# A two-layer FFT mixer and feed-forward kernel on one core: changed end wait, FFN rows 2 and 3 in half-height matmuls, smaller evictions and loads, and a new hand-made order

## Chip, cores and metric

The kernel runs on one core of one Trainium2 chip. The metric is the device time of one execution in microseconds, as the median of several runs. TensorE is PE in the profile, VectorE is DVE, ScalarE is ACT, GpSimdE is POOL, and SyncE is SP, which here issues nearly all the DMAs.

## What is computed

`x` has 2048 tokens of 448 features in bf16. Two identical layers follow one another, each a spectral mixing step and a feed-forward step:

```python
def _A_ref(x, w_r, w_i):
    X = rfft2(x.astype(float32), axes=(-2, -1))
    X = X * (w_r + 1j * w_i)
    return irfft2(X, s=(S, D), axes=(-2, -1)).astype(bfloat16)

def _B_ref(x, w1, b1, w2, b2):
    h = einsum("bsd,df->bsf", x, w1) + b1          # 448 -> 1792
    h = where(h > 0, h, 0) ** 2
    return einsum("bsf,fd->bsd", h, w2) + b2       # 1792 -> 448

x = x + _A_ref(layernorm(x), w_r, w_i)
x = x + _B_ref(layernorm(x), w1, b1, w2, b2)
x = x + _A_ref(layernorm(x), w_r, w_i)
x = x + _B_ref(layernorm(x), w1, b1, w2, b2)
```

The layer norms have no learned scale. The weights are the same in both layers and stay in SBUF.

## The kernel before

**Tiles and stages.** The 2048 tokens are 16 tiles of 128 rows, `x_sb[:, t, :]`, with row p*16+t in partition p. All transforms are matmuls with constant matrices that are loaded from DRAM (`TD`, `G`, `H`, `TI`, `FI`, `FA`, `J`). A layer runs through these stages, and the tag of each is the name used in the text:

- **A1.t / A2.t** (first layer / second layer, tile t). Statistics for the layer norm (`ln_stats`), the cosine/sine matrix scaled by 1/std (`scaled` into `Fs`), four matmuls, and an eviction of the PSUM bank (128x512) to `XA` (`A_out`). In A1 the input comes from `xin`, which is loaded in the pieces listed in `XLOADS`. In A2 the input tile is x as the first layer leaves it. It is folded first into sums and differences (`tt` into `xin`, then into `yA`), so that each of the four matmuls takes 112 of the folded columns.
- **TD.p**, p from 1 to 15 and then 0: four matmuls (in layer 2 four times 112 wide) that need `XA` of all 16 tiles, and an eviction.
- **B.p**: three matmuls of 448 columns with `G_sb[:, p]`, eviction to `EF`.
- **W.p**: the complex product with the spectral weights `Wt` on DVE, as one multiplication into `tmp`, one subtraction and one sum into `Z`, for one p or two at once.
- **Bi.p**: four matmuls of 128 rows and 256 columns with `H_sb[:, p]`, eviction to `VT`. TI of any tile needs all 16 of them.
- **TI.t, AI.t**: the last inverse transform, per tile, and its addition to `x_sb`.
- **ln.t, xbln.t**: square and square root on ACT, then the tile is transposed to `yT` for the FFN. Tiles 0 and 1 are transposed on PE with a permutation matrix `J_sb` (`flip`). The others go by a DMA transpose. Tiles 0 to 3 are not normalised: the raw x is transposed, the mean and the standard deviation ride along in two more columns, which meet two rows b1 in `W1_sb`, and the result is scaled by `r2` afterwards. Tiles 4 to 15 are normalised into `xn` (`scaled`, and a copy `cp` of the last 64 columns) and then transposed.
- **h.c.t0**: the first FFN matmul of chunk c (four tiles). Chunk 0 is done in two parts of two tiles each by `h_part`: per block of 128 hidden features (14 blocks) four matmuls of 128 rows and 256 columns. Chunks 1 to 3 are done by `h_pairs`: every 128-row block is cut into two halves of 64 rows, of which two at a time run side by side in the upper and the lower half of the array. The 448 input features are seven halves per block of hidden features, so 98 halves a chunk with N=512. The last 64 rows of W1 must stand in the upper partitions for that. They are loaded again into `W1u`. Then squared ReLU: ACT does ReLU with the bias `b1col`, DVE squares.
- **o.t**: 14 matmuls of 448 columns and one DVE instruction that adds the residual. Tile 15 is done in two column parts in layer 1 (`CUT`, 224 and 224) and three in layer 2.
- **Output**: a DMA per tile or part, issued by SP. At its end the program waits for each of SP's DMA semaphores. SP's DMAs use 20 semaphores in turn.

**What sets the order.** The code records operations in units, and `ORDER`, a table written by hand, gives each unit its rank. A letter behind the rank (a, d, p) gives the engine. Each engine then executes its own list in rank order and waits on semaphores where an operand isn't ready yet, so an early instruction that waits holds all that stand behind it on its engine. This holds for SP too: a DMA that waits for its target buffer to be free holds every DMA behind it.

**Lines.** In the trace of before all matmuls are L637, activations L656, evictions L662 (ACT) and L663 (DVE), `scaled` L673/L674, DVE two-input operations L689, copies L693, DMAs L628, DMA transposes L623, statistics L788 to L795, the addition in AI L938, the square L962, the output of o L1060, and the filler matmuls that keep TensorE's clock up L1153. The waits at the end are L1166.

## Time and profile before

| | us |
|---|---|
| median of 3 runs | 258.3 |
| lowest, highest | 258.0, 259.23 |
| the profiled execution, its time | 258.49 |
| the profiled execution, span of the trace | 256.7 |
| PE busy | 247.8 (97%) |
| DVE busy | 203.1 (79%) |
| ACT busy | 167.5 (65%) |
| granted TensorE clock | 1.00 |

The trace covers one execution. Its time is 1.8 us more than its span, since the time has work ahead of and behind the recorded instructions in it. A row of the timeline gives start, length, engine, line, and operation, then out<-in with shapes, and how many such instructions in a row it stands for. In square brackets is the idle time ahead of it and what ended it. The trace shortens names, so that `W_sb` is W1_sb or W2_sb and `in_B_b_dram` is b1 or b2. SPq is SP's sequencer, which issues DMAs.

### The profile page before, as it was taken

How to read it: one execution, taken by the hardware profiler on the slowest of the kernel's cores; microseconds unless marked ns; L12 is line 12 of the kernel's file. 1: busy time of each engine (PE TensorE's matmuls, PEld its weight loads, DVE VectorE, ACT ScalarE, POOL GpSimd, SP SyncE). 2: the span in 40 equal slices, each digit the busy share in tenths (PEclk: the TensorE clock that was granted, in tenths of full speed). 3: DMA queues.
4: the chain of work that ended last, by engine and by line, in shares of the span. 5: the costliest groups of instructions: out<-in, count | busy, mean ns of one | idle time of the engine just before them, and what ended most of it. 6: DMA issues, size and time to landing. Idle time of an engine off the chain costs nothing.

```text
span 256.7 us, 5442 instructions
## 1 busy us (share of the span) xinstructions
PE 247.8 (97%) x2025; PEld 155.0 (60%) x2025; DVE 203.1 (79%) x622; ACT 167.5 (65%) x397; POOL 6.5 (3%) x18
## 2 busy tenths in 40 slices
...
GB/s 235 308 181 307 174 224 6 99 233 36 44 3 40 43 43 72 4 0 0 3 0 3 1 3 0 3 43 43 42 72 3 41 63 106 46 3 0 58 38 67
DMA packets 30397, 17.25 MB, mean 67 GB/s; under 512 B 23170, under 2 KB 28898, under 8 KB 30372
## 3 DMA queue, kind: packets, MB, share of 16 engines
...
## 4 chain that ended last, share of the span: by engine, by line
PE 80%; ACT 12%; DVE 3%; DMA 3%; issue 1%; SPq 0%; POOL 0%
PE ps L637 79%; ACT arena L662 5%; ACT VT L662 5%; DMA xin<-in_A_x_dram 3%; ACT tmp L662 1%; DVE x_sb L938 1%; DVE XA L663 1%; SPq L628 0%; ACT VT L962 0%; DVE Fs L674 0%; DVE tmp L663 0%; DVE st L788 0%; PE ps L1153 0%; DVE x_sb L1060 0%; POOL Fs L674 0%
## 5 line engine op out<-in xcount | busy, mean ns | idle before, releaser
L637 PE MATMUL ps<-yT,W_sb 64*128 64x512 bf16 (+1 forms) x770 | 89.8, 346 | 0.0
L637 PE MATMUL ps<-W_sb,arena 128*128 128x448 bf16 (+2 forms) x490 | 87.5, 336 | 0.0
L637 PEld LDWEIGHTS ps<-yT,W_sb 64*128 64x128 bf16 (+1 forms) x770 | 50.7, 95 | 36.9 <-issue 1.5
L637 PEld LDWEIGHTS ps<-W_sb,arena 128*128 128x128 bf16 x490 | 46.2, 98 | 36.7 <-DVE arena L689 1.0
L656 ACT ACTIVATE arena<-ps,b1col 128x512 bf16<-128x512 f32 x84 | 52.3, 691 | 19.3 <-PE ps L637 19.1
L689 DVE TENSOR_TENSOR arena<-arena 128x512 bf16<-128x512 bf16 (+1 forms) x140 | 45.4, 368 | 14.1 <-ACT arena L656 13.9
L962 ACT ACTIVATE VT<-x_sb 128x448 bf16<-128x448 bf16 x32 | 18.3, 574 | 15.5 <-DVE x_sb L938 15.4
L662 ACT ACTIVATE arena<-ps 128x448 bf16<-128x448 f32 x54 | 25.5, 608 | 2.7 <-PE ps L637 2.7
L1060 DVE SCALAR_TENSOR_TENSOR x_sb<-ps,arena 128x448 bf16<-128x448 f32 (+2 forms) x27 | 15.3, 570 | 14.6 <-PE ps L637 14.3
L656 ACT ACTIVATE mv<-mv,epst 128x1 f32<-128x1 f32 (+1 forms) x46 | 13.0, 296 | 13.6 <-DVE mv L789 12.9
L656 ACT ACTIVATE arena<-ps 128x256 bf16<-128x256 f32 x56 | 17.6, 397 | 0.8 <-PE ps L637 0.7
L689 DVE TENSOR_TENSOR tmp<-arena,Wt 128x1792 bf16<-128x1792 bf16 (+1 forms) x20 | 17.7, 903 | 0.2
L637 PE MATMUL ps<-H_sb,arena 128*128 128x256 bf16 x128 | 15.8, 272 | 0.3 <-ACT VT L662 0.3
L637 PE MATMUL ps<-yT,VT 64*128 64x512 bf16 x42 | 15.8, 376 | 0.0
L637 PE MATMUL ps<-arena,G_sb 128*128 128x224 bf16 (+1 forms) x96 | 15.7, 290 | 0.0
L662 ACT ACTIVATE XA<-ps 128x512 bf16<-128x512 f32 x28 | 15.0, 607 | 1.0 <-PE ps L637 0.8
L662 ACT ACTIVATE VT<-ps 128x512 bf16<-128x512 f32 (+2 forms) x28 | 14.6, 808 | 0.0
L637 PEld LDWEIGHTS ps<-H_sb,arena 128*128 128x128 bf16 x128 | 11.7, 98 | 3.2 <-DVE arena L689 0.8
L637 PE MATMUL ps<-TD_sb,XA 128*128 128x224 bf16 (+1 forms) x128 | 12.1, 236 | 0.9 <-DVE XA L663 0.7
L689 DVE TENSOR_TENSOR arena<-tmp 128x448 bf16<-128x448 bf16 (+1 forms) x40 | 11.7, 341 | 0.1
L938 DVE SCALAR_TENSOR_TENSOR x_sb<-ps,mv,x_sb 128x448 bf16<-128x448 f32 x16 | 10.7, 679 | 1.3 <-PE ps L637 1.3
L637 PE MATMUL ps<-TI_sb,VT 112*128 112x112 bf16 (+1 forms) x128 | 9.7, 224 | 1.8 <-ACT VT L662 1.5
...
## 6 DMA issues: line engine op xcount, KB each, us to landing
out_dram<-x_sb SPq DMA_DIRECT2D x15, 112.0 KB, 1.8
...
G_sb<-c_G SPq DMA_DIRECT2D x3, 480.0 KB, 6.1
H_sb<-c_H SPq DMA_DIRECT2D x3, 480.0 KB, 8.8
...
```

The source lines that it names most:

```text
L637: return sch.add("pe", lambda e: e.matmul(_res(o), lhsT, rhs, start=start, stop=stop, skip_group_check=skip), [lhsT, rhs], [o], cost=cost, ...
L656: sch.add("act", lambda e: e.activation(o, _res(i), func, **kw), rd, [o], cost=c)
L662: op = sch.add(engs[0], lambda e: e.activation(o, _res(i), ACT.Copy) if h[0].eng == "act" else e.tensor_copy(o, _res(i)), [i], [o], cost=c ...
L663: e.tensor_copy(o, _res(i)), [i], [o], cost=c[engs[0]], unit=unit)
L689: sch.add(eng, lambda e: e.tensor_tensor(o, _res(a), b, op), [a, b], [o], cost=_free(o) / rate + 69.0)
L938: small(lambda e, xx=xx, xi=xi, r=r, m=m: e.scalar_tensor_tensor(out=xx, in0=_res(r), scalar=m, in1=xi, op0=ALU.subtract, op1=ALU.add), [r ...
L962: sch.add("act", lambda e, i=i, o=o, x=x: e.activation(o, x, ACT.Square, accum_out=mv[:, i, 4:5]), [x], [o, mv[:, i, 4:5]], cost=560.0)
L1060: small(lambda e: e.scalar_tensor_tensor(out=o, in0=_res(i), scalar=r[0] if r else 1.0, in1=xb[:, t, d0:d1], op0=ALU.mult, op1=ALU.add), [ ...
```

## The change

1. **End.** The semaphores of the DMAs are awaited in the order of their last use, so the last transfer is awaited last. Before, they were awaited by index, and the last transfer's was the twelfth of 20.
2. **FFN rows 2 and 3** (the second half of chunk 0). In both layers `h_pairs` is used for them (`NORM0 = (2, 2)`), with N=256. So 98 halves of 64 rows take the place of 56 matmuls of 128 rows. Tiles 2 and 3 are normalised for that like tiles 4 to 15. The upper copy of the last W1 rows comes from a new DMA of 64x1792 into `XA[64:128]` (`W1f`), once per layer. `XA` is read by all TD of the layer before it is free.
3. **Tile 15 in A2.** The output of layer 1 for tile 15 comes in 336 and 112 columns instead of 224 and 224 (`LAST`). The second fold of this tile is done on TensorE (`PFOLD`), and the first fold is cut into pieces of 112 columns.
4. **Evictions.** Those to `XA` of tiles 12 to 15 (layer 1) and of 13 and 15 (layer 2) are cut into two halves. Those to `VT` for some p are cut into a part for 4 tiles and a part for 12, which may come later (`A_CUT`, `BI_CUT`). Before, the latter was done for p=0 alone.
5. **W.** In layer 2 the sum is left out for p = 11 to 15 and 0 (`NOZI`): two sums of two p and two of one p. Bi multiplies the two addends one after the other with the same `H_sb`, so that it has six matmuls instead of four for these six p, 12 matmuls of 256 columns more.
6. **Loads and small buffers.** x is loaded in smaller pieces over the queues of SP and ACT. `J_sb` has a tile of its own, and some small tiles are merged.
7. **Order.** The whole of `ORDER` is new.

In the diff below only the entries of Bi0.0 and TI0.0 in `ORDER` are left, and the passing on of arguments is left out.

```diff
-XLOADS = (("sp", ((0, 1, 3300.0), (2, 4, 4450.0), (4, 6, 5900.0), (8, 12, 7500.0))),
-          ("act", ((None, None, 3150.0), (1, 2, 4600.0), (6, 8, 6100.0), (12, 16, 8500.0))))
+XLOADS = (("sp", ((0, 1, 3200.0), (2, 4, 4700.0), (4, 6, 5950.0), (8, 10, 7200.0), (12, 14, 8700.0))),
+          ("act", ((None, None, 3000.0), (1, 2, 4850.0), (6, 8, 6150.0), (10, 12, 7400.0), (14, 16, 8900.0))))
 NP = 16
-BI_CUT = (0,)
+BI_CUT = ((0, 10, 12, 13), (0, 3, 10, 11))
+NORM0 = (2, 2)
+A_CUT = ((12, 13, 14, 15), (13, 15))
+LAST = 336
+PFOLD = (15,)
+NOZI = ((), (11, 13, 15, 0))
...
-    "Bi0.0": "264 265a 270a", "TI0.0": "267 268d 269 271d 279 280a 272 274d", "AI0.0": "277 278",
...
+    "Bi0.0": "275 276a 278a", "TI0.0": "279 280a 281 282d 293 294d 286 287a", "W1f0": "223", "AI0.0": "285 288",
...
+        W1f = XA[:].rearrange("p a b c t j -> p (a b c t j)")[:, 0:2048].rearrange("p (k c) -> p k c", k=4)
...
-        J_sb = x_sb[:, 4:6, D:4 * P]
+        J_sb = sb("J_sb", [P, P])
...
-        def evac(o, i, engs=("act", "dve"), unit=None):
+        def evac(o, i, engs=("act", "dve"), unit=None, after=None):
...
+            if after is not None:
+                op.deps.append(after)
+                op.gdeps.append(after)
...
-        def A_out(t, q, engs):
-            src = q[lambda b: ps[:, b, :].rearrange("p (k c j) -> p k c j", k=4, c=2 * NP)]
-            dst = XA[:, :, :, :, t, :].rearrange("p k g c j -> p (k g) c j")
-            evac(dst, src, engs)
+        def A_out(t, q, engs, cut):
+            prev = None
+            for a, b in ((0, NP), (NP, 2 * NP)) if cut else ((0, 2 * NP),):
+                src = q[lambda x, a=a, b=b: ps[:, x, :].rearrange("p (k c j) -> p k c j", k=4, c=2 * NP)[:, :, a:b]]
+                dst = XA[:, :, :, a:b, t, :].rearrange("p k g c j -> p (k g) c j")
+                evac(dst, src, engs, after=prev)
+                prev = sch.last_write[_pages(dst)[0]]
...
-            tt(z[:, :, 1], T[:, :, 0, 1], T[:, :, 1, 0], ALU.add)
+            if p in NOZI[L]:
+                for k in range(n):
+                    parts[L, p + k] = (T[:, k, 0, 1], T[:, k, 1, 0])
+            else:
+                tt(z[:, :, 1], T[:, :, 0, 1], T[:, :, 1, 0], ALU.add)
...
-                for h in range(2):
-                    mm(q[lambda b, lb=lb: ps[:, b, lb * 256:(lb + 1) * 256]], Z[:, p, h, lb:256:2],
-                       H_sb[:, p, P * (1 - h):P * (1 - h) + 256], h == 0, h == 1, skip=True)
+                mm(q[lambda b, lb=lb: ps[:, b, lb * 256:(lb + 1) * 256]], Z[:, p, 0, lb:256:2], H_sb[:, p, P:P + 256],
+                   True, False, skip=True)
+                zs = parts.get((L, p), (Z[:, p, 1],))
+                n = QD if len(zs) == 2 else P
+                for i, z in enumerate(zs):
+                    mm(q[lambda b, lb=lb, n=n: ps[0:n, b, lb * 256:(lb + 1) * 256]], z[:, lb:2 * n:2], H_sb[:, p, 0:256],
+                       False, i == len(zs) - 1, skip=True)
...
-            for a, b in ((0, 4), (4, NT)) if p in BI_CUT else ((0, NT),):
-                evac(VT[:, :, :, a:b, 2 * p:2 * p + 2, :].rearrange("p a g t c j -> p (a g) t (c j)"),
-                     q[lambda b0, a=a, b=b: ps[:, b0, :].rearrange("p (k t c) -> p k t c", k=4, t=NT)[:, :, a:b]], EV["Bi"])
+            prev = None
+            for a, b in ((0, 4), (4, NT)) if p in BI_CUT[L] else ((0, NT),):
+                dst = VT[:, :, :, a:b, 2 * p:2 * p + 2, :].rearrange("p a g t c j -> p (a g) t (c j)")
+                evac(dst, q[lambda b0, a=a, b=b: ps[:, b0, :].rearrange("p (k t c) -> p k t c", k=4, t=NT)[:, :, a:b]], EV["Bi"],
+                     after=prev)
+                prev = sch.last_write[_pages(dst)[0]]
...
-            if t < 4:
+            if plain:
...
-                for i in range(n):
-                    scaled(xn[:, i, 0:D], x_sb[:, t + i, 0:D], rstd[:, t + i, 0:1], EV["XN"])
-                cp(xn[:, 0:n, D:4 * P], xn[:, 0:n, 3 * P:D])
-                dma("sp", yT[:, t:t + n, :, :].rearrange("p t k c -> p (t k) c"),
-                    xn[:, 0:n, :].rearrange("p t c -> p (t c)"), transpose=True, lat=2000.0 if t == 4 and not last else 400.0)
+                for i in range(t, t + n):
+                    scaled(xn[:, i % 2, 0:D], x_sb[:, i, 0:D], rstd[:, i, 0:1], EV["XN"])
+                    if t < NFLIP:
+                        flip(i, 1, 0, 4, lambda i: xn[:, i % 2, :])
+                if t >= NFLIP:
+                    cp(xn[:, 0:n, D:4 * P], xn[:, 0:n, 3 * P:D])
+                    dma("sp", yT[:, t:t + n, :, :].rearrange("p t k c -> p (t k) c"),
+                        xn[:, 0:n, :].rearrange("p t c -> p (t c)"), transpose=True, lat=2000.0 if t == 4 and not last else 400.0)
...
-        def h_pairs(c):
-
-            tk = slice(4 * c, 4 * c + 4)
+        def h_pairs(c, t0, t1, W1u):
+
+            tk, w = slice(4 * c + t0, 4 * c + t1), (t1 - t0) * P
...
-                w = W1u[h, fb // 4, fb % 4 * P:(fb % 4 + 1) * P] if up and j == 3 else W1_sb[h, j, f]
-                op = mm(q[fb][lambda b: ps[:, b, :]], w, yT[h, tk, j, :], start, stop, unit=u)
+                s = W1u[h, fb // 4, fb % 4 * P:(fb % 4 + 1) * P] if up and j == 3 and max(NORM0) else W1_sb[h, j, f]
+                op = mm(q[fb][lambda b: ps[:, b, 0:w]], s, yT[h, tk, j, :], start, stop, unit=u)
...
-                    hb = hbuf[c % 2][:, fb, :]
-                    act(hb, q[fb][lambda b: ps[:, b, :]], ACT.Relu, bias=b1col[:, fb:fb + 1])
+                    hb = hbuf[c % 2][:, fb, t0 * P:t1 * P]
+                    act(hb, q[fb][lambda b: ps[:, b, 0:w]], ACT.Relu, bias=b1col[:, fb:fb + 1])
...
+            n = 2 * P if t in PFOLD else P
+            f = Fs[:, t % NFS, 0:n]
+            scaled(f, FA_sb[:, 0:n], rstd[:, t, 0:1], EV["FS2"])
             q = _Tile(1)
-            for k in range(2):
+            for g in range(2) if t in PFOLD else ():
+                w = xin[:, t, g * HD:(g + 1) * HD]
+                for k, (a, m) in enumerate(((w[:, 0:QD], f[:, None, 0:P].to_broadcast([P, 2, P])),
+                                            (w[:, QD:HD], f.rearrange("p (k c) -> p k c", k=2)))):
+                    mm(q[lambda b, g=g: ps[0:QD, b, :].rearrange("p (k g c) -> p g k c", k=2, g=2)[:, g]], a, m,
+                       k == 0 and g == 0, k == 1 and g == 1, skip=True)
+            for k in range(2) if t not in PFOLD else ():
                 for g in range(2):
                     d = (2 * k + g) * QD
                     mm(q[lambda b, d=k * 2 * P + g * P: ps[:, b, d:d + P]], yA[:, t % 8, d:d + P], f,
                        k == 0 and g == 0, k == 1 and g == 1, skip=True)
-            A_out(t, q, EV["A2"])
+            A_out(t, q, EV["A2"], t in A_CUT[1])
...
-        CUT = ((0, HD), (HD, D)) if HALVES else ((0, D),)
+        CUT = ((0, LAST), (LAST, D)) if HALVES else ((0, D),)
...
+            if NORM0[L] < 4 and max(NORM0):
+                sch.tag = f"W1f{L}"
+                dma("sp", XA[64:128].rearrange("p a b c t j -> p (a b c t j)")[:, 0:FF], B_w1[384:448, :])
...
+                    if t0 >= NORM0[L]:
+                        h_pairs(c, t0, t1, W1f)
+                        continue
...
+                        for i in (1, 0) if t in PFOLD or t == NT - 1 and LAST > HD else (2,):
+                            if i and t in PFOLD:
+                                a, b = x[:, HD - 1:QD - 1:-1], x[:, HD:HD + QD]
+                            else:
+                                lo, hi = ((0, QD), (QD, HD), (0, HD))[i]
+                                a, b = x[:, lo:hi], x[:, D - 1 - lo:D - 1 - hi:-1]
+                            lo, hi = ((0, QD), (QD, HD), (0, HD))[i]
+                            for g in range(2):
+                                tt(w[:, g, lo:hi], a, b, ALU.subtract if g else ALU.add)
+                        for k in range(2) if t not in PFOLD else ():
...
-            for j in range(_Sched.NDSEM[ename]):
-                fin = sch.final[(ename, True, j)]
-                if fin > 0:
-                    need((ename, True, j), fin)
+            last = {op.dsem: i for i, op in enumerate(sch.ops[ename]) if op.is_dma}
+            for j in sorted(last, key=last.get):
+                need((ename, True, j), sch.final[(ename, True, j)])
```

Three places of the engines' lists follow, before and after. On SP, the DMAs around the second half of the loads of constants; `H_sb` 128x1920 is H for five p, `H_sb` 128x384 H for p=0, `XA<-in_B_w1_dram` the new load. Before:

```order
L628 DMA x_sb<-c_J 128x2x64
L628 DMA Wt<-in_A_w_r_dram 64x6x224
L628 DMA H_sb<-c_H 128x384
L628 DMA G_sb<-c_G 128x1920
...
L628 DMA H_sb<-c_H 128x1920 x3
L628 DMA b1in<-in_B_b1_dram 128x14x1
L628 DMA W1_sb<-in_B_b1_dram 1x1792
L628 DMA Wt<-in_A_w_i_dram 64x224
L628 DMA Wt<-in_A_w_r_dram 64x224
L628 DMA x_sb<-in_B_b2_dram 128x7x64
L628 DMA W1_sb<-in_B_w1_dram 128x3x1792
```

After:

```order
L634 DMA XA<-in_B_w1_dram 64x1792
L634 DMA W1_sb<-in_B_b1_dram 1x1792
L634 DMA Wt<-in_A_w_r_dram 64x224
L634 DMA H_sb<-c_H 128x1920
L634 DMA b1in<-in_B_b1_dram 128x14x1
L634 DMA x_sb<-in_B_b2_dram 128x7x64
L634 DMA J_sb<-c_J 128x128
L634 DMA H_sb<-c_H 128x384
L634 DMA W1_sb<-in_B_w1_dram 128x3x1792
L634 DMA W2_sb<-in_B_w2_dram 128x14x448
```

H for p=0 and J have moved from ahead of the G loads to behind b2row, the third H load stands by itself, and all of these stand behind the new load, which needs `XA` free.

On PE, the first FFN matmuls of rows 2 and 3 in layer 1 and what follows. `yT,W1_sb` is an h matmul, `tmp,FI_sb` and `TI_sb,VT` are stages of TI of later tiles, and `W2_sb,arena` is o. Before:

```order
L637 MATMUL ps<-tmp,FI_sb 128x2x112 x4
L637 MATMUL ps<-yT,W1_sb 128x256 x48
L637 MATMUL ps<-TI_sb,VT 128x112 x8
L637 MATMUL ps<-yT,W1_sb 128x256 x20
L637 MATMUL ps<-tmp,FI_sb 128x2x112 x4
L637 MATMUL ps<-W2_sb,arena 128x448 x28
```

After:

```order
L643 MATMUL ps<-yT,W1_sb 128x256 x16
L643 MATMUL ps<-tmp,FI_sb 128x2x112 x4
L643 MATMUL ps<-yT,W1_sb 128x256 x7
L643 MATMUL ps<-yT,XA 128x256
L643 MATMUL ps<-yT,W1_sb 128x256 x7
L643 MATMUL ps<-yT,XA 128x256
L643 MATMUL ps<-yT,W1_sb 128x256 x13
...
L643 MATMUL ps<-yT,W1_sb 128x256 x12
L643 MATMUL ps<-TI_sb,VT 128x112 x8
L643 MATMUL ps<-W2_sb,arena 128x448 x14
```

The matmuls with `XA` are the halves on the upper copy of W1. In this layer, the first, the 98 halves stand in one piece.

On ACT, the end of A2, with the last evictions to `XA` and the first of TD. Before:

```order
L662 ACTIVATE XA<-ps 128x128x4 x2
L656 ACTIVATE mv<-mv,epst 128x1
L662 ACTIVATE XA<-ps 128x128x4 x4
L662 ACTIVATE arena<-ps 128x448 x23
```

After:

```order
L668 ACTIVATE XA<-ps 128x128x4 x2
L662 ACTIVATE mv<-mv,st 128x1
L668 ACTIVATE XA<-ps 128x128x4 x3
L668 ACTIVATE XA<-ps 128x4x16x4 x4
L668 ACTIVATE arena<-ps 128x448 x24
```

The four half evictions are those of tiles 13 and 15, and they now stand behind the whole ones.

81 lines of the change are left out of this document (44 added, 37 removed), and 192 rows, old and new, of the table ORDER.

## The prediction

> **What bounds the kernel now.** I first read the busy times by engine over the whole span, then the chain that ended last, and then cut the span where the chain changes engine. The stage table has per engine the busy time and in brackets its instructions.
>
> ```profile
> core 0: us, PE busy (x) PEld busy (x) DVE busy (x) ACT busy (x) POOL busy (x), PEclk, DMA share, GB/s
> 0.00:17.47 17.47, 14.34 (x84) 7.90 (x84) 13.99 (x50) 13.77 (x38) 6.48 (x18) 1.00 0.83 250
> 17.47:37.47 20.00, 19.41 (x176) 16.83 (x177) 18.64 (x38) 18.38 (x41) 0.00 (x0) 1.00 0.80 237
> 37.47:135.66 98.19, 97.85 (x796) 58.59 (x797) 84.15 (x292) 61.68 (x151) 0.00 (x0) 1.00 0.18 42
> 135.66:139.38 3.72, 3.01 (x32) 1.72 (x29) 2.14 (x13) 3.33 (x8) 0.00 (x0) 1.00 0.00 0
> 139.38:158.22 18.84, 17.62 (x178) 13.24 (x179) 17.84 (x38) 18.25 (x41) 0.00 (x0) 1.00 0.01 2
> 158.22:253.91 95.69, 95.59 (x766) 56.76 (x766) 66.11 (x190) 52.12 (x121) 0.00 (x0) 1.00 0.18 41
> 253.91:256.70 2.79, 0.00 (x0) 0.00 (x0) 0.28 (x1) 0.00 (x0) 0.00 (x0) 1.00 0.12 31
> ```
>
> The rows are: the head (loads, A1), TD to Bi of the first layer, its inverse and FFN with A2 beside, the end of A2, TD to Bi again, the second FFN, and the last output. In the two FFN rows only PE is full: 97.85 of 98.19 us and 95.59 of 95.69. There only fewer or shorter matmuls count. In the two spectral rows PE, ACT and DVE are all above 90%, so shortening one alone frees little. In the head and at the end of A2 no engine is full, and latencies in a row set the time. The clock is 1.00 all through.
>
> **Head: smaller loads, halved evictions.** DVE does the statistics as the tiles arrive.
>
> ```profile
> 8.57 0.63 DVE L788 BATCH_NORM_STATS2 st<-xin 128x6 f32<-128x448 bf16 x1 [0.62 <-DMA xin<-in_A_x_dram]
> 15.34 1.88 DVE L663 CAST XA<-ps 128x512 bf16<-128x512 f32 x3
> 17.47 1.69 PE L637 MATMUL ps<-TD_sb,XA 128*128 128x224 bf16 x16 [0.72 <-DVE XA L663]
> ```
>
> At 8.57 DVE has waited 0.62 us for one transfer of tiles 8 to 11. Two pieces over two queues give the first two tiles earlier, and this wait goes: −0.6. At the end three whole evictions in a row hold TD back until 17.47. With tiles 12 to 15 in halves, the TD whose p lies in the first half of the channels can start one half of a 0.63 us cast earlier: −0.3 to −0.4. I take −1.0 together. The bounds are −1.2 (both and a bit of the 0.72) and −0.3 (the evictions alone, if what follows the statistics on POOL and PE is no earlier).
>
> **Loads of constants: the new load stands ahead of H.** This is the part that speaks against the change. Let L be the end of the last TD of the first layer.
>
> ```profile
> 27.40 0.55 PE L637 MATMUL ps<-TD_sb,XA 128*128 128x224 bf16 x4
> 32.75 4.13 PE L637 MATMUL ps<-H_sb,arena 128*128 128x256 bf16 x36
> ```
>
> L is about 27.8 here, the end of the row at 27.40 but for the overlap. The 36 matmuls take 4.13 us, 0.109 us each after the first. The last Bi, p=0, is the last four of them and starts at 32.75 + 32×0.109 = 36.24, which is L+8.45. It needs H of p=0, which in the new order comes only after `XA` is free, so after L, and behind seven other transfers. When would it land?
>
> ```profile
> 24.29 3.42 SPq L628 DMA_DIRECT2D W_sb<-in_B_b_dram  x1
> 27.76 0.59 SPq L628 DMA_DIRECT2D Wt<-in_A_w_i_dram  x1
> 29.44 0.60 SPq L628 DMA_DIRECT2D x_sb<-in_B_b_dram  x1
> 30.08 0.55 SPq L628 DMA_DIRECT2D W_sb<-in_B_w_dram  x1
> 32.00:34.00 2.00, 2.00 (x20) 1.74 (x19) 2.00 (x6) 2.00 (x5) 0.00 (x0) 1.00 0.24 57
> 34.00:36.00 2.00, 2.00 (x21) 1.68 (x19) 1.94 (x7) 2.00 (x6) 0.00 (x0) 1.00 0.93 363
> x_sb<-in_B_b_dram SPq DMA_DIRECT2D x1, 112.0 KB, 6.4
> out_dram<-x_sb SPq DMA_DIRECT2D x2, 28.0 KB, 1.5
> b1in<-in_B_b_dram SPq DMA_DIRECT2D x1, 3.5 KB, 10.4
> H_sb<-c_H SPq DMA_DIRECT2D x3, 480.0 KB, 8.8
> ```
>
> The rows with a start are SP's issues, then two windows, then transfers with KB and us from issue to landing. SP issues the new load, the b1 row and Wt at about 0.6 us each, and then H for five p at L+1.9. A small transfer takes 1.5 us from issue to landing (28 KB row), and 480 KB at 363 GB/s 1.3 us more: L+4.7. b1in is 3.5 KB in 1792 single elements, and I put 1.2 us for it (estimate: its 10.4 us are mostly the three H ahead of it). b2row then holds the queue. It is broadcast to 128 rows and lands 6.4 us after its issue at 29.44, and while it runs the queue moves 57 GB/s although W1 is queued behind it since 30.08. Only from 34 on do 363 GB/s flow. So it blocks about 3.6 us (from 29.44 + 1.5 = 30.9 to 34.5). J and H of p=0 add 0.35, and the slowest of the 16 engines 0.4. The sum is L+10.2. Against a need at L+8.45 PE stalls **1.7 us** at the last Bi, and TI and all after it with it. Bounds: 0, if b1in and b2row run beside each other and the H load, and 2.9, if b1in costs 2.4. H for five p lands at L+4.7 and has cover: its first use is the tenth of the 16 Bi, 24 matmuls ahead of the last, at 8.45 − 24×0.109 = L+5.8.
>
> W1 follows H0. 1344 KB at 363 GB/s are 3.7 us, so about L+13.9, or 40.7 with L a us earlier. The first FFN matmul comes at 43.77 −1.0 +1.7, so this is covered by 3.8 us. W2, now ahead of the first transpose on SP's queue, adds 1568 KB or 4.3 us: about 45, before that transpose is issued (46.71 in the trace below).
>
> **Rows 2 and 3 in halves.** In h_pairs of the full width:
>
> ```profile
> 68.61:79.29 10.68, 10.68 (x99) 4.72 (x99) 8.38 (x26) 7.81 (x16) 0.00 (x0) 1.00 0.01 2
> 77.90 1.46 PE L637 MATMUL ps<-yT,W_sb 64*128 64x512 bf16 x12
> 79.29 0.56 PE L637 MATMUL ps<-tmp,FI_sb 128*128 128x224 bf16 x4
> 49.33 5.40 PE L637 MATMUL ps<-yT,W_sb 128*128 128x256 bf16 x48
> 46.71 1.34 SPq L623 DMA_TRANSPOSE yT<-x_sb  x1
> yT<-x_sb SPq DMA_TRANSPOSE x2, 3.2
> ```
>
> 98 halves of 512 columns take 10.68 us, 0.109 each, so of 256 columns 0.0545 if all of it halves, and 98 take 5.34. The 56 whole ones take 56×0.109 = 6.10. That is −0.76 a layer. Each change between halves and whole rows costs about 0.08: 77.90 + 12×0.109 = 79.21, and the next starts at 79.29. The first layer gets two more such changes and the second four, since there a piece of TI stands inside. −0.76×2 + 6×0.08 = −1.04. A part per instruction will not halve (2 ns on 98 halves are 0.2 a layer), so I take **−0.8** (bounds −1.1 and 0).
>
> Tiles 2 and 3 now need a reciprocal, two scalings and a copy ahead of their transpose, about 0.8 us more than a copy and a subtraction. In before the transpose was issued at 46.71 and landed 3.2 us later, at 49.9. Its first use comes after 12 matmuls of the row at 49.33, at 50.6. This 0.7 and the TI matmuls that are now placed ahead cover it: nothing. If they don't, 0.3. The cast to `b1col`, now needed in the first chunk, needs b1in at L+6, two us before TI: nothing.
>
> **End of A2, tile 15.**
>
> ```profile
> 135.91 1.08 ACT L662 ACTIVATE XA<-ps 128x512 bf16<-128x512 f32 x2
> 137.06 2.06 ACT L662 ACTIVATE XA<-ps 128x512 bf16<-128x512 f32 x4
> 139.97 0.54 ACT L662 ACTIVATE arena<-ps 128x448 bf16<-128x448 f32 x1 [0.85 <-PE ps L637]
> L656 ACT ACTIVATE arena<-ps 128x256 bf16<-128x256 f32 x56 | 17.6, 397 | 0.8 <-PE ps L637 0.7
> L662 ACT ACTIVATE XA<-ps 128x512 bf16<-128x512 f32 x28 | 15.0, 607 | 1.0 <-PE ps L637 0.8
> 139.38 1.54 PE L637 MATMUL ps<-TD_sb,XA 112*128 112x112 bf16 x28 [0.18 <-issue]
> ```
>
> DVE's new fold (fewer steps in a row for tile 15) would help little, because ACT is what ends last: it evicts without a gap from 135.91 to 139.12, 0.515 us apart, and TD starts at 139.38. A half costs 397 against 607 ns, 210 less, so about 0.305. The second halves of 13 and 15 can wait: two halves ahead of TD in place of two wholes give 2×0.21 = **−0.4**. The deferred 0.6 us fall into ACT's 0.85 us of idle time before 139.97. If TD soon wants the second half, that comes back: bounds −0.7 and +0.2.
>
> **Spectral part, second layer.** The sums left out:
>
> ```profile
> L689 DVE TENSOR_TENSOR arena<-tmp 128x448 bf16<-128x448 bf16 x24 | 8.4, 388 | 0.0
> L689 DVE TENSOR_TENSOR arena<-tmp 128x224 bf16<-128x224 bf16 x16 | 3.9, 271 | 0.1
> ```
>
> The groups' busy times give two of 8.4/24 = 0.35 and two of 3.9/16 = 0.24 us: DVE −1.2. PE gets 12×0.109 = +1.3. The stage lasts 18.84 us, with ACT at 18.25, PE at 17.62 and DVE at 17.84. ACT, the fullest, does the same work, and PE would be at 18.9 with the 12 matmuls if nothing else gave: **0** (bounds −0.5 and +0.7).
>
> **End.**
>
> ```profile
> L628 SPq DMA_DIRECT2D out_dram<-x_sb x5: 332/332/432, 249.9 to 254.2; - x5
> L1166 SPq EVENT_SEMAPHORE  x9: 28/28/28, 255.7 to 256.2; - x9
> ```
>
> The last DMA, issued at 254.2, lands 1.5 us later at 255.7. Then nine waits follow until 256.2. In the new order eight of the nine run earlier, under the transfer: 8/9 of 0.5, **−0.5** when rounded. If these waits were not sequential after landing it would be 0.
>
> **Sum.** −1.0 + 1.7 − 0.8 + 0 − 0.4 + 0 − 0.5 = −1.0 against the profiled execution's 258.49: 257.5. That execution lies 0.19 above the median, so **257.3**. A measurement of this kernel can tell about 0.5%, 1.3 us, from no change: faster starts below 257.0 and slower above 259.6. Main case, 60%: between 256.2 and 258.4, with a little over a third of it below 257.0.
>
> **Rivals.**
>
> *The loads are in time* (25%): the transfers of small elements run beside others, H of p=0 lands by L+8.5, no stall. 257.3 − 1.7 = 255.6. For it: the queue's 16 engines each take their share, and in before b1in's own cost isn't visible. Against it: the window from 32 to 34, in which W1 hardly moves behind b2row.
>
> *The queue jams* (10%): in the trace the issue of the b1 row at 24.29 took 3.42 us instead of about 0.6. The same 3.5 KB transfer stands right behind the new load in the new order. If it holds SP again, all behind it is 3.1 us later: stall 4.8, **260.4**, slower than before. It decides from a stall of 4.2 us on (257.3 + 2.5 = 259.8). Against it: at 24.29 the DMA share was near full with three H loads queued, of which one is now later.
>
> *Short halves are bound by their weights* (5%): each half loads its own 64x128 weights.
>
> ```profile
> L637 PEld LDWEIGHTS ps<-yT,W_sb 64*128 64x128 bf16 x546 | 29.0, 94 | 34.3 <-issue 1.5
> ```
>
> If one needed the 94 ns of a load by itself, 98 halves would take 9.2 us, +3.1 on the 6.10 in each layer, and 6.2 + 0.5 for the changes of rows + 0.8 for the gain that is then missing give 257.3 + 7.5 = **264.8**. It decides as soon as a load blocks more than 62 ns, 6.10/98. Against it stand the 28 TD matmuls at 139.38, 112 columns each with their own load: 1.54 us, at most 55 ns from one to the next. The Trainium skill, page "TensorE: Matmul & The Clock Gate", section "LDWEIGHTS (loading the stationary operand)", gives a load about P/1.2 ns, by my estimate 107 ns for 128 columns, and by it the halves would take 10.5 us. The 55 ns of the row disagree with that as a spacing, so this rival gets no more than its 5%.
>
> **How the numbers follow.** Faster: all of the second case and 0.35 of the first, 0.25 + 0.21 = 0.46. Slower: the last two, less a fifth of the jam, 0.13. Same: the rest, 0.41. The range leaves out about one in ten on each side: from 255.0 (loads in time, head at its bound) to 259.4 (main case with the longer stall of 2.9 and halves that gain nothing).
>
> **What would show it.** In the profile after, at the last four `H_sb` matmuls of the first layer PE should be idle 1 to 2.5 us, released by the DMA of H. If there is no gap, the second case holds. If the issue behind the `XA` load takes over 2 us, it is the jam. The 98 halves should take 5.3 to 5.6 us (9 in the last rival). TD of the second layer should start at about 139.38 − 1.0 + 1.7 − 0.3 − 0.4 = 139.4, and eight of the final waits should lie before the last landing. I am wrong in the main if PE's stage from TD to TI in the first layer stays at 20.0 us or less.

## The result and the profile after

The changed kernel takes **257.06 us** (median of 8 runs, 256.62 to 257.64), the kernel before on the same chips 258.32. The ratio is 0.9937, with a 95% interval of 0.9909 to 0.9965. The forecast was 257.3. The change made the kernel about 0.6% faster, just short of what the prediction called "faster" (below 257.0). The profiled execution took 257.33 us, with a span of 255.40.

The stage table of the changed kernel, cut at the same events as that of before (start of TD, start of TI, last evictions of A2, and so on):

```profile
core 0: us, PE busy (x) PEld busy (x) DVE busy (x) ACT busy (x) POOL busy (x), PEclk, DMA share, GB/s
0.00:17.09 17.09, 14.91 (x85) 7.93 (x85) 13.19 (x50) 13.42 (x39) 6.88 (x19) 1.00 0.84 253
17.09:37.31 20.22, 19.55 (x176) 16.73 (x177) 18.87 (x42) 18.51 (x44) 0.00 (x0) 1.00 0.73 198
37.31:134.90 97.59, 97.37 (x837) 57.06 (x838) 83.91 (x291) 64.44 (x153) 0.00 (x0) 1.00 0.20 52
134.90:138.40 3.50, 2.74 (x32) 1.92 (x29) 2.12 (x14) 3.48 (x10) 0.00 (x0) 1.00 0.03 7
138.40:156.94 18.54, 17.95 (x189) 15.15 (x190) 17.74 (x35) 18.37 (x45) 0.00 (x0) 1.00 0.05 14
156.94:253.09 96.15, 95.60 (x808) 55.74 (x808) 65.60 (x185) 54.47 (x126) 0.00 (x0) 1.00 0.16 40
253.09:255.40 2.31, 0.00 (x0) 0.00 (x0) 0.28 (x1) 0.00 (x0) 0.00 (x0) 1.00 0.29 87
```

Row by row against before, in us:

| stage | before | after | difference | forecast |
|---|---|---|---|---|
| head, to TD | 17.47 | 17.09 | −0.38 | −1.0 |
| TD to TI, first layer | 20.00 | 20.22 | +0.22 | +1.7 |
| TI, FFN and A2 to TD of the second layer | 101.91 | 101.09 | −0.82 | about −0.85 (halves and A2) |
| TD to TI, second layer | 18.84 | 18.54 | −0.30 | 0 |
| TI and FFN, second layer | 95.69 | 96.15 | +0.46 | about −0.35 (halves) |
| end | 2.79 | 2.31 | −0.48 | −0.5 |
| sum | 256.70 | 255.40 | −1.30 | −1.0 |

The sum agrees much better than its terms do. The head and the second FFN came out 0.62 and 0.81 above their forecasts, TD to TI of the first layer 1.48 below its forecast and that of the second 0.30 below.

**The load that was to stall TensorE.** PE around the last Bi of the first layer, and SP's issues from the load into `XA` on:

```profile
30.64 5.40 PE L643 MATMUL ps<-H_sb,arena 128*128 128x256 bf16 x48
36.35 0.60 PE L643 MATMUL ps<-H_sb,arena 128*128 128x256 bf16 x4 [0.31 <-DVE VT L669]
37.31 1.33 PE L643 MATMUL ps<-TI_sb,VT 112*128 112x224 bf16 x16 [0.37 <-ACT VT L668]
```

```profile
27.57 0.48 SPq L634 DMA_DIRECT2D XA<-in_B_w_dram  x1
28.15 0.39 SPq L634 DMA_DIRECT2D W_sb<-in_B_b_dram  x1
28.63 0.47 SPq L634 DMA_DIRECT2D Wt<-in_A_w_r_dram  x1
29.16 0.59 SPq L634 DMA_DIRECT2D H_sb<-c_H  x1
29.80 0.42 SPq L634 DMA_DIRECT2D b1in<-in_B_b_dram  x1
30.26 1.49 SPq L634 DMA_DIRECT2D x_sb<-in_B_b_dram  x1
31.79 1.28 SPq L634 DMA_DIRECT2D J_sb<-c_J  x1
33.12 1.47 SPq L634 DMA_DIRECT2D H_sb<-c_H  x1
```

There is a gap before the last Bi, as forecast, but of 0.31 us instead of 1.7 (0.47 by the starts, since a matmul starts before the one ahead of it has ended). The profile names an eviction by DVE as what ended it. H of p=0, issued at 33.12, landed on the last DMA engine at 36.26, 3.1 us later, and the matmul starts at 36.35. The runs of h_before_xa and h_after_w1 below decide between the two.

**The halves of rows 2 and 3**, first in the first layer, then around the piece of TI in the second:

```profile
49.98 0.55 PE L643 MATMUL ps<-tmp,FI_sb 128*128 128x224 bf16 x4
50.47 0.61 PE L643 MATMUL ps<-yT,W_sb 64*128 64x256 bf16 x7
...
55.17 0.82 PE L643 MATMUL ps<-yT,W_sb 64*128 64x256 bf16 x12
55.92 0.57 PE L643 MATMUL ps<-TI_sb,VT 112*128 112x112 bf16 x8
...
172.18 0.49 PE L643 MATMUL ps<-yT,W_sb 64*128 64x256 bf16 x6
172.70 0.54 PE L643 MATMUL ps<-tmp,FI_sb 128*128 128x224 bf16 x4
173.08 1.14 PE L643 MATMUL ps<-yT,W_sb 128*128 128x256 bf16 x11
```

In the first layer all halves stand between 50.47 and 55.92, 5.45 us for 98, against 6.10 for the 56 whole ones. Two of them start 3 ns apart, and such pairs follow one another at 109 ns, which is 0.0545 us each, as the rows of before gave for half the columns. A change between whole rows and halves, a change of height in what follows, costs 0.096 us: the first half starts 192 ns after the last FI matmul, which follow one another at 96. In the second layer the row at 173.08 is a mixture: four whole matmuls of rows 0 and 1, and then halves again. So there are four changes of height.

**End of A2 and end of the program.** ACT's evictions, and the issues and waits of SP before and after:

```profile
136.05 2.64 ACT L668 ACTIVATE XA<-ps 128x512 bf16<-128x512 f32 x7
138.79 1.53 ACT L668 ACTIVATE arena<-ps 128x448 bf16<-128x448 f32 x3
```

```profile
L634 SPq DMA_DIRECT2D out_dram<-x_sb x4: 332/333/333, 251.7 to 253.4; - x4
L1226 SPq EVENT_SEMAPHORE  x13: 17/28/28, 252.1 to 254.9; - x13
```

The row at 136.05 holds wholes and halves. TD starts at 138.40 while the deferred halves are still running. At the end the last transfer is issued at 253.4, and the last wait is over at 254.9, 1.5 us later. That is the landing itself, with nothing behind it. Before, 0.5 us of waits followed.

**The head.** A wait of DVE for x and the start of TD, both of the changed kernel:

```profile
6.48 0.63 DVE L800 BATCH_NORM_STATS2 st<-xin 128x6 f32<-128x448 bf16 x1 [0.62 <-DMA xin<-in_A_x_dram]
17.09 1.79 PE L643 MATMUL ps<-TD_sb,XA 128*128 128x224 bf16 x17 [0.68 <-ACT XA L668]
```

The wait of before at 8.57 is gone, but there is one of the same length at 6.48, for an earlier piece of x. The experiments below, which share this head, show how much of it is chance.

**A wait in the second FFN.** What PE waited for from the second TI on, and SP around the last transpose:

```profile
PE ps L643 <- DVE VT L669: 0.6, 1, 0.6
PE ps L643 <- DVE x_sb L698: 0.3, 1, 0.3
PE ps L643 <- DMA yT<-arena: 0.2, 1, 0.2
```

```profile
215.52 0.81 SPq L634 DMA_DIRECT2D out_dram<-x_sb  x2
216.45 2.54 SPq L629 DMA_TRANSPOSE yT<-arena  x1
```

The transpose of the last two tiles is issued behind two output transfers and takes SP 2.54 us (the one at 46.71 in before took 1.34). The pairs of the last chunk wait for it at 220.96. From the last pair of the third chunk 542 ns pass instead of 213, a loss of 0.33 us.

### The profile page after: what moved, and what is told of

Same layout as the page of the kernel before. It is cut to its first block, busy times and chain, and to the rows that moved or that the text cites. A ratio compares the mean times of both kernels' runs of the same rounds, so it can differ in the third digit from the quotient of the medians.

```text
span 255.4 us, 5649 instructions
## 1 busy us (share of the span) xinstructions
PE 248.1 (97%) x2120; PEld 154.5 (61%) x2120; DVE 201.7 (79%) x615; ACT 172.7 (68%) x411; POOL 6.9 (3%) x19
## 4 chain that ended last, share of the span: by engine, by line
PE 80%; DVE 8%; ACT 5%; DMA 4%; issue 1%; SPq 1%; DVEq 0%
PE ps L643 80%; DVE tmp L698 2%; DMA xin<-in_A_x_dram 2%; ACT XA L668 2%; DMA yT<-arena 2%; DVE arena L698 1%; ACT arena L668 1%; DVE tmp L669 1%; DVE st L800 1%; ACT mv L662 1%; DVE VT L669 1%; DVE x_sb L966 1%; SPq L634 1%; ACT arena L662 0%; DVE x_sb L1097 0%
## 5 line engine op out<-in xcount | busy, mean ns | idle before, releaser
L643 PE MATMUL ps<-yT,W_sb 64*128 64x512 bf16 (+2 forms) x840 | 89.2, 339 | 0.2 <-DMA yT<-arena 0.2
L643 PE MATMUL ps<-W_sb,arena 128*128 128x448 bf16 (+3 forms) x490 | 87.2, 337 | 0.0
L662 ACT ACTIVATE arena<-ps,b1col 128x512 bf16<-128x512 f32 (+1 forms) x112 | 63.2, 636 | 22.4 <-PE ps L643 22.1
L643 PEld LDWEIGHTS ps<-yT,W_sb 64*128 64x128 bf16 (+1 forms) x840 | 49.2, 94 | 37.5 <-issue 2.7
L1097 DVE SCALAR_TENSOR_TENSOR x_sb<-ps,arena 128x448 bf16<-128x448 f32 (+3 forms) x31 | 17.6, 574 | 16.1 <-PE ps L643 15.8
L662 ACT ACTIVATE mv<-mv,st 128x1 f32<-128x1 f32 (+1 forms) x46 | 12.5, 291 | 12.3 <-DVE mv L801 11.2
L668 ACT ACTIVATE XA<-ps 128x512 bf16<-128x512 f32 (+1 forms) x31 | 14.9, 547 | 4.5 <-PE ps L643 4.5
L668 ACT ACTIVATE tmp<-ps 128x896 bf16<-128x896 f32 (+1 forms) x13 | 10.3, 814 | 1.3 <-PE ps L643 1.3
L643 PE MATMUL ps<-TI_sb,VT 112*128 112x112 bf16 (+1 forms) x128 | 10.2, 224 | 1.0 <-DVE VT L669 0.6
L643 PEld LDWEIGHTS ps<-arena,G_sb 128*128 128x128 bf16 x96 | 8.9, 98 | 3.2
L966 DVE SCALAR_TENSOR_TENSOR x_sb<-ps,mv,xin 128x448 bf16<-128x448 f32 x16 | 10.4, 678 | 0.4 <-PE ps L643 0.3
## 6 DMA issues: line engine op xcount, KB each, us to landing
W_sb<-in_B_w_dram SPq DMA_DIRECT2D x1, 1568.0 KB, 10.2
```

What stands on the lines that cost most here:

```text
L643: return sch.add("pe", lambda e: e.matmul(_res(o), lhsT, rhs, start=start, stop=stop, skip_group_check=skip), [lhsT, rhs], [o], cost=cost, ...
L662: sch.add("act", lambda e: e.activation(o, _res(i), func, **kw), rd, [o], cost=c)
L668: op = sch.add(engs[0], lambda e: e.activation(o, _res(i), ACT.Copy) if h[0].eng == "act" else e.tensor_copy(o, _res(i)), [i], [o], cost=c ...
L966: small(lambda e, xx=xx, xi=xi, r=r, m=m: e.scalar_tensor_tensor(out=xx, in0=_res(r), scalar=m, in1=xi, op0=ALU.subtract, op1=ALU.add), [r ...
L1097: small(lambda e: e.scalar_tensor_tensor(out=o, in0=_res(i), scalar=r[0] if r else 1.0, in1=xb[:, t, d0:d1], op0=ALU.mult, op1=ALU.add), [ ...
```

## The experiments

My theory after comparing the traces: the sum came out right because the wait for H was much smaller than priced, while the head gave less and the second FFN lost what its halves gained. The main rival: the parts whose stages got shorter are not the cause, and the new order alone is. Each kernel is the changed one with one thing undone or moved; where units change, the edit also gives them ranks in `ORDER`, most of which the diffs below leave out. The table gives stage lengths in us, all read from the traces: from start to start of the first matmuls of TD, TI and o, except that "last o→TD" begins at the end of the last o matmul and "o→last matmul" ends with the end of the last.

| kernel | time, median | TD starts | TD→TI | TI→o, layer 1 | last o→TD | TD→TI, layer 2 | TI→o, layer 2 | o→last matmul | end |
|---|---|---|---|---|---|---|---|---|---|
| before | 258.3 | 17.47 | 20.00 | 20.06 | 3.73 | 18.84 | 19.37 | 76.31 | 2.80 |
| changed | 257.06 | 17.09 | 20.23 | 19.01 | 3.46 | 18.54 | 19.89 | 76.25 | 2.32 |
| end_by_index | 257.5 | 16.84 | 20.26 | 19.01 | 3.45 | 18.54 | 19.89 | 75.95 | **2.62** |
| h_before_xa | 257.12 | 16.85 | **19.97** | 19.01 | 3.45 | 18.54 | 19.88 | 76.55 | 2.31 |
| h_after_w1 | 262.72 | 17.55 | **25.06** | 18.99 | 3.46 | 18.54 | 19.88 | 75.95 | 2.31 |
| rows23_whole | 259.39 | 16.58 | 20.25 | **19.56** | 3.46 | 18.54 | **20.06** | **77.31** | 2.31 |
| a2_as_before | 257.66 | 16.69 | 20.29 | 19.01 | **4.40** | 18.54 | 19.89 | 75.95 | 2.32 |
| a2_evict_whole | 257.33 (one run) | 16.61 | 20.15 | 19.01 | **3.88** | 18.54 | 19.90 | 76.51 | 2.32 |
| xa_whole | 257.77 | **17.95** | 20.17 | 19.01 | 3.45 | 18.54 | 19.89 | 75.95 | 2.31 |
| x_loads_big | 257.98 | **18.09** | 20.21 | 19.01 | 3.45 | 18.54 | 19.89 | 75.95 | 2.31 |
| head_as_before | 257.3 (one run) | **17.51** | 20.13 | 19.01 | 3.46 | 18.54 | 19.90 | 76.03 | 2.32 |
| w_sums_back | 257.45 | 16.48 | 20.39 | 19.01 | 3.45 | **18.96** | 19.86 | 76.03 | 2.32 |
| ffn2_order | 258.83 | 16.60 | 20.05 | 19.01 | 3.46 | 18.54 | **22.12** | 75.95 | 2.32 |
| both_orders | 258.69 | 16.61 | **19.97** | 19.01 | 3.46 | 18.54 | **22.12** | 75.95 | 2.31 |

Where nothing was edited, a stage comes back to within 0.01 to 0.05 us. Three columns vary more by themselves: the start of TD (16.5 to 17.1, once 17.55), TD→TI of the first layer (20.05 to 20.39), and o→last matmul, which takes 75.95 or up to 0.6 more. So effects of 0.2 to 0.5 us, which the times of a few runs can't separate, can be read from the other columns. The times were taken beside kernel before at 258.24 to 258.55, so differences of 0.3 us between two rows of that column say little.

Not in the table is the stretch from the first to the last o of layer 1: 78.11 in before, 78.62 in the changed kernel and all others but h_after_w1 (79.12) and rows23_whole (79.11). Part of the 0.51 is work that moved: four matmuls of TI that stood ahead of the first o in before now stand behind it. In layer 2 four went the other way, which is 0.38 of the growth of its TI→o.

**end_by_index** puts the old waits back:

```diff
-            last = {op.dsem: i for i, op in enumerate(sch.ops[ename]) if op.is_dma}
-            for j in sorted(last, key=last.get):
-                need((ename, True, j), sch.final[(ename, True, j)])
+            for j in range(_Sched.NDSEM[ename]):
+                fin = sch.final[(ename, True, j)]
+                if fin > 0:
+                    need((ename, True, j), fin)
```

> Only the order of the waits at the end goes back to the index of the semaphore. If the end is worth what the trace shows (2.79 us from the last matmul to the end before, 2.31 after), this stage comes back to about 2.8 us, and the time rises by 0.5 us to about 257.5. Rival: the waits cost nothing by themselves and the shorter end comes from the last transfer being faster; then the stage stays at 2.3 us.

The end is 0.30 us longer, 2.62 against 2.32. Its last transfer is issued at 252.9 and would be down at 254.4; the last wait ends at 254.7:

```profile
L634 SPq DMA_DIRECT2D out_dram<-x_sb x18: 332/363/577, 189.4 to 252.9; - x18
L1226 SPq EVENT_SEMAPHORE  x13: 17/28/28, 251.6 to 254.7; - x13
```

The waits are sequential work behind the landing, as the prediction had it. It is 0.3 and not 0.5 us because the new program issues 75 DMAs on SP instead of 72, so that its last transfer has the fifteenth of the 20 semaphores instead of the twelfth, with five behind it instead of eight: about 0.06 us each in both cases.

**h_before_xa** and **h_after_w1** move H of p=0 on SP's queue, the first with J to ahead of the load into `XA`, the second to behind W1:

```diff
+ORDER["sp.J_sb"] = "222.4"
+ORDER["sp.H_sb"] = "183 182 228 222.5"
```

```diff
+ORDER["sp.H_sb"] = "183 182 228 270.5"
```

> J and H of p=0 are issued ahead of the load that waits for XA. If the 0.31 us of idle TensorE ahead of the last Bi of the first layer is the wait for H (it landed at 36.26, the matmul starts at 36.35, and the trace names an eviction by VectorE that ended at 36.03), the gap shrinks by about 0.2 us and TI starts 0.2 us earlier, at 37.1. Rival: the eviction was what it waited for, or the evictions behind it set TI anyway; then TI starts at 37.3 as before.

> H of p=0 goes behind the 1344 KB of W1 on the queue. If PE waits for this load at the last Bi, and nothing behind it catches up, H lands at about 40.5, the last Bi starts about 4.2 us later than in the changed kernel, and the time rises by about 4 us to 261. This is the size of a late H that the prediction's rival of a jam was priced by. Rival: the FFN stage has slack that takes up part, and the time rises by under 3 us.

PE at the last Bi, first of h_before_xa and then of h_after_w1:

```profile
30.40 5.97 PE L645 MATMUL ps<-H_sb,arena 128*128 128x256 bf16 x52
36.82 1.33 PE L645 MATMUL ps<-TI_sb,VT 112*128 112x224 bf16 x16 [0.45 <-ACT VT L670]
```

```profile
34.04 2.78 PE L644 MATMUL ps<-H_sb,arena 128*128 128x256 bf16 x24 [0.16 <-DVE tmp L699]
36.66 2.98 PE L1214 MATMUL ps<-ones 128*128 128x512 bf16 x13
41.58 0.60 PE L644 MATMUL ps<-H_sb,arena 128*128 128x256 bf16 x4 [1.94 <-DMA H_sb<-c_H]
```

With H early the 52 matmuls run in one piece and TD→TI takes 19.97, 0.26 less than in the changed kernel. The profile's releaser, the eviction, was wrong; it had ended 0.2 us before H landed. With H late (it landed at 41.44) the last Bi starts at 41.58, named as a wait for H, and the time rises by 5.7 us over the changed kernel's. 4.8 of that are the stage; another 0.5 is a wait of the pairs of the first layer at 106.62, where two pairs start 708 ns apart instead of 213, and TD started late (17.55). So the place is as critical as the prediction had it, and a late H is paid in full; only how late H comes was wrong. The estimate of +4 us was low, since W1 landed at 41.17 and H behind it, 0.9 later than expected, and since the late start of TD and the wait of the pairs were not in it.

**rows23_whole** undoes the halves:

```diff
-NORM0 = (2, 2)
+NORM0 = (4, 4)
```

and gives the entries of `ORDER` for these rows (`h0.0.2`, `h1.0.2`, `ln0.2`, `ln1.2` and their `xb`) the ranks of the units they replace.

> Rows 2 and 3 go back to 56 matmuls of 128 rows in both layers, with the raw x transposed and no load into XA. By the prices in the trace (98 halves of 0.0545 us and 0.096 us for each change of height) the halves are worth 0.57 us in the first layer and 0.38 in the second, where a piece of TI and four whole matmuls stand between them: the time rises by 0.95 less what the load into XA costs (0.2), to about 257.8. Rival: the halves' gain is lost again in waits in both layers, and the time stays at 257.1 within 0.2.

The two stretches that hold rows 2 and 3 are longer, by 0.55 us in the first layer (theory 0.57) and 0.17 in the second (theory 0.38). But the time rises by 2.3 us, far above either number. The rest lies elsewhere: in the first layer a new gap of 0.49 us stands at 79.53, behind the first o, and in the second layer o→last matmul takes 77.31 instead of 75.95, with two new gaps (0.73 and 0.49 us), of which the first is

```profile
183.24 0.35 PE L649 MATMUL ps<-W_sb,arena 128*128 128x448 bf16 x1
184.15 2.06 PE L649 MATMUL ps<-W_sb,arena 128*128 128x448 bf16 x10 [0.57 <-DVE arena L704]
```

PE waits there for squares by DVE, which stand in the order where the halves had wanted them. A table of ranks fits one set of operations. So the price of the halves is read from their own stretch, not from the total.

**a2_as_before** undoes the pieces of tile 15 and the evictions, **a2_evict_whole** the evictions alone:

```diff
-A_CUT = ((12, 13, 14, 15), (13, 15))
-LAST = 336
-PFOLD = (15,)
+A_CUT = ((12, 13, 14, 15), ())
+LAST = 224
+PFOLD = ()
```

```diff
-A_CUT = ((12, 13, 14, 15), (13, 15))
+A_CUT = ((12, 13, 14, 15), ())
```

> Tile 15 of A2 goes back to 224 and 224 columns, the second fold to VectorE, and the evictions to XA in the second layer are whole again. If cutting the last evictions is what lets TD start earlier there, the stretch from the last output of the first layer to TD of the second grows by 0.3 to 0.4 us, and the time with it, to about 257.4. Rival: VectorE's fold ended last and ACT was full only by chance; then undoing the fold costs more, 0.6 us or over.

> Only the cut of the evictions of tiles 13 and 15 in the second layer is undone; the unequal pieces and the fold on TensorE stay. Undoing all three cost 0.94 us from the last output matmul to TD (4.40 instead of 3.46). If the prediction's reading holds that the evictions on ScalarE end last there, and a half for a whole saves 0.2 us each, most of it comes back: 0.4 us, so 3.86 us. Rival: the fold on VectorE is what counted, and it stays below 3.6.

The evictions alone are worth 0.42 us (3.88 against 3.46), the term of the sum and the mechanism, since in a2_evict_whole TD starts 0.2 us behind the last eviction:

```profile
135.50 2.53 ACT L670 ACTIVATE XA<-ps 128x512 bf16<-128x512 f32 x5
138.28 0.90 PE L645 MATMUL ps<-TD_sb,XA 112*128 112x112 bf16 x15 [0.20 <-ACT XA L670]
```

All three together are worth 0.94, so the pieces and the fold on TensorE are worth 0.52 more in this order. That contradicts the step by which the new fold "would help little", and the traces show how. Both kernels end with five whole evictions without a gap, and ahead of these ACT takes the square root for the norm of tile 15. In a2_as_before it waits 0.53 us for DVE's statistics there, in a2_evict_whole 0.02, since the last o and its statistics take 112 columns instead of 224. So the first of the five starts 1.63 us after the last o instead of 1.10. That points at the pieces, not the fold; no run undoes the fold alone. With the kernel before's own order the same stretch took 3.73, not 4.40, so some of the 0.94 is again an order that no longer fits.

**xa_whole**, **x_loads_big** and **head_as_before** undo the cut evictions of the first layer, the small loads of x, and both:

```diff
-A_CUT = ((12, 13, 14, 15), (13, 15))
+A_CUT = ((), (13, 15))
```

```diff
-XLOADS = (("sp", ((0, 1, 3200.0), (2, 4, 4700.0), (4, 6, 5950.0), (8, 10, 7200.0), (12, 14, 8700.0))),
+XLOADS = (("sp", ((0, 1, 3300.0), (2, 4, 4450.0), (4, 6, 5900.0), (8, 12, 7500.0))),
...
```

> The last evictions to XA in the first layer are whole again, the loads of x stay small. If the halves let TD start early, TD starts 0.3 to 0.4 us later than 17.09. Rival: TD's start is set by when the last x tiles arrive and get through the statistics, and it moves by under 0.1 us.

> x is loaded in the large pieces of before, the evictions stay cut. The prediction had the small pieces at 0.6 us, but the head became only 0.38 us shorter. If the small pieces are worth what they were priced at, TD starts 0.6 us later than 17.09. Rival: the head is bound behind the loads by ACT, which evicts without a gap from 14.2 to 16.8, and TD starts less than 0.2 us later.

> Large loads of x and whole evictions together, in the new order. Each alone made TD start about 1.1 us later than the mean of 16.9 of the kernels with the new head. If the two prices are of separate waits, TD starts at about 19.1. Rival: both lie on one chain, of which the later end counts, and TD starts at about 18.1. In the kernel before, with the order made for it, it started at 17.47.

DVE's waits for x, in xa_whole, x_loads_big and head_as_before:

```profile
7.04 1.15 DVE L802 BATCH_NORM_STATS2 st<-xin 128x6 f32<-128x448 bf16 x2 [1.17 <-DMA xin<-in_A_x_dram]
```

```profile
5.81 1.15 DVE L800 BATCH_NORM_STATS2 st<-xin 128x6 f32<-128x448 bf16 x2 [0.29 <-DMA xin<-in_A_x_dram]
9.35 0.63 DVE L800 BATCH_NORM_STATS2 st<-xin 128x6 f32<-128x448 bf16 x1 [1.61 <-DMA xin<-in_A_x_dram]
```

```profile
6.35 1.16 DVE L802 BATCH_NORM_STATS2 st<-xin 128x6 f32<-128x448 bf16 x2 [0.19 <-DMA xin<-in_A_x_dram]
```

None of the numbers expected for the third came true: both undone cost less than each alone. The rows say why. When x arrives varies from run to run, and TD moves with it. Among the kernels with the new head, those with at most 0.14 us of such a wait start TD at 16.48 to 16.61, those with a wait of 0.22, 0.37, 0.62 and 0.96 us at 16.69, 16.85, 17.09 and 17.55: about 16.5 plus the wait. By this line xa_whole with 1.17 us would be at 17.6 to 17.7, and it is at 17.95. By this estimate the cut evictions are worth about **0.3 us**, and the rest is the wait, which lies ahead of them. x_loads_big has a wait of 1.61 us for the large piece of tiles 8 to 11, of which head_as_before, with the same loads, has 0.06 (at 8.34). The large pieces risk this wait and don't always pay it.

The line rests on one profile of each kernel, and the spans of the other executions leave room for more: their median is 255.9 us in xa_whole, no shorter than in the profiled execution, and 255.6 in x_loads_big, against 255.15 in the changed kernel. So that the wait in xa_whole was chance is not shown, and what each of the two parts is worth on average is left open.

**w_sums_back** gives the six sums back to VectorE:

```diff
-NOZI = ((), (11, 13, 15, 0))
+NOZI = ((), ())
```

> The six sums of the second layer are back on VectorE and the 12 matmuls of TensorE are gone. The prediction had this at nothing. The stage from TD to TI was 18.84 us before and is 18.54 us in the changed kernel, of which the sums could be the cause: then it grows to about 18.8. Rival: the new order is the cause, and the stage stays at 18.5 or gets shorter, down to 17.9, since TensorE has 1.3 us less to do.

The stage, from the start of TD to that of TI:

```profile
137.94:156.91 18.97, 18.07 (x180) 13.46 (x181) 18.34 (x39) 18.51 (x45) 0.00 (x0) 1.00 0.05 13
```

It is 0.42 us longer, with DVE at 18.34 instead of 17.74 and ACT, the fullest engine in both, hardly changed (18.51 and 18.37). In this order the sums account for that stage's gain of 0.30 over before, and more. Taking work from DVE helped although DVE was not the fullest by its busy time, and the 12 matmuls more were hidden. A likely reason is that three engines, each busy for over 95%, wait for one another through DVE's products; no run shows that by itself.

**ffn2_order** and **both_orders** try to repair the second FFN: the piece of TI and the whole matmuls out of the halves, tile 15's square and transpose earlier; the second also has H early.

```diff
+ORDER["AI1.6"] = "1049 1024 1050 1051 1057 1058.1 1058.2"
+ORDER["ln1.14"] = "1223 1223.1 1223.2 1249.1 1249.2d 1249.3d 1249.4 1249.5"
```

with ranks 1057 and 1058.5 for the last block of `h1.0.0` and its eviction.

> Only ranks in the second layer: the piece of TI and the four whole matmuls between the halves of rows 2 and 3 go ahead of them, and the square, scaling and transpose of tile 15 are ranked earlier. Two changes of height fewer at 0.096 us: the stretch from TI to the first output matmul gets 0.2 us shorter, from 19.89 to 19.7, and the wait for the last transpose (0.33 us in the trace of the changed kernel, absent in most of the other runs) is gone, 75.95 us from there to the last matmul. Rival: what is moved ahead waits for its own operands there, and the stretch stays at 19.9 or grows.

> The ranks of the second layer and the early J and H of p=0 together. The early H was worth 0.28 us from TD to TI (19.97 instead of 20.25), the other 0.2 to 0.5 if it holds: 0.5 to 0.8 us below the changed kernel, about 256.5. Rival: the second part gives nothing, 256.8.

The rival held, and worse than it said: TI→o of layer 2 took 22.12 us instead of 19.89. PE in that stretch of ffn2_order:

```profile
170.63 0.77 PE L646 MATMUL ps<-tmp,FI_sb 128*128 128x224 bf16 x4 [0.80 <-DVE tmp L701]
171.24 1.14 PE L646 MATMUL ps<-yT,W_sb 128*128 128x256 bf16 x11
...
178.02 0.54 PE L646 MATMUL ps<-tmp,FI_sb 128*128 128x224 bf16 x4 [0.73 <-ACT arena L665]
```

The piece of TI isn't ready where it was put: what DVE writes into `tmp` ends 0.8 us too late for the row shown, and ahead of that gap PE has already run matmuls on `ones`, which only fill the time. Where it had stood, between the halves, it cost two changes of height (0.19 us) and saved a wait of over 1 us. The earlier transpose did take away the wait of the last chunk (75.95), but so did chance in most of the other kernels. The early H kept its gain (19.97). No version beat the changed kernel: h_before_xa is within the measurement's uncertainty of it, 257.12 against 257.06, ratio to before 0.9955 with an interval of 0.9937 to 0.9972.

## Why the prediction was right

The time was right within 0.3 us, and partly by luck: not all terms were right, and their errors happened to cancel. By its own sign PE was to be idle for 1 to 2.5 us at the last Bi; it was idle for 0.31. So the mechanism is nearer to the first rival, by which the loads are in time and the kernel takes 255.6, and the time is not, because the head of the profiled execution and the second FFN came out 0.6 and 0.8 above their forecasts.

- **Wait for H: right place, wrong size.** 1.7 us were forecast; the runs show 0.26 to 0.31. The step that failed is "So it blocks about 3.6 us": b2row. With L = 27.41, the end of the last TD but for the overlap, H of p=0 landed at L+8.9 instead of L+10.2. A transfer is spread over 16 engines, and the trace has a landing from each. By the ninth of the 16, H for five p was down at 32.84 (L+5.4, forecast 4.7), b1in 1.4 us later at 34.22 (forecast 1.2), b2row 0.8 us after that at 35.01 (forecast 3.6), and J and H of p=0 another 1.0 later (forecast 0.35). In before the same count gives b2row 3.66.

  Two things shortened it. Its 896 pieces of 128 bytes ran from 32.92 on, ahead of the landing of b1in, so the two overlapped, as the lower bound of that term had it. And they took 2.4 us from the first to the last, against 4.8 in before. The traces of all kernels point to what stands behind b2row on the queue: W1 does in before, h_before_xa and both_orders, and there the pieces took 4.8, 3.7 and 4.8 us; in the other eleven it is the small J, and they took 2.3 to 3.1. The prediction took the length from before, with W1 behind. Why W1 there makes it longer is open. How long SP needs for the issue doesn't sort the cases: 1.49 us in the changed kernel, 1.24 in both_orders, 0.82 in head_as_before, 0.60 in before.
- **Head: about right, but blurred by arrival.** −1.0 was forecast, −0.38 came. The new head without a wait for x is at 16.5 to 16.6, 0.9 before the 17.47 of before, and the profiled execution lost 0.6 of that to a late piece of x. The 17.47 has a wait of that length too, but head_as_before, which has only 0.06 us of it, starts at 17.51, so the 0.9 stands in the new order, on one execution. The share of the cut evictions, 0.3 to 0.4 by the forecast, is about 0.3 by the line above.
- **Halves: right.** The rate of 0.0545 us and the 5.45 us for 98 are as worked out; the changes of height cost 0.096 instead of 0.08. −0.8 was forecast; undoing them lengthened their own stretches by 0.55 and 0.17, together 0.72. The rival of a bound by weight loads is refuted: one load per 0.0545 us. On a change between halves and whole rows, the Trainium skill, page "TensorEngine Tiling (Array Packing)", section "Key Properties", says that TensorE drains. The 0.096 us lost at each change fit that; that draining is their cause is not shown here.
- **End of A2: right for the evictions** (0.42 measured, 0.4 forecast), wrong for the fold and the unequal pieces, which were put at nothing and measured 0.52 in the new order.
- **Second spectral part: wrong.** 0 was forecast, −0.3 came, and undoing the sums cost 0.42. The step "ACT, the fullest, does the same work" took busy time for the bound. The range given for the term, −0.5 to +0.7, held it.
- **Second FFN: wrong by 0.8.** The four changes were priced. What was missed is a wait ahead of the flips (0.3 us for x_sb, where before has none of that length) and the wait for the last transpose, 0.33 in this execution; in others the stretch is shorter by 0.3 or longer by up to 0.3. The two make up 0.6 of the 0.8.
- **End: right**, −0.48 for −0.5.
- The **jam** did not occur: the issue behind the load into `XA` took 0.39 us. But h_after_w1 shows that a late H is paid in full, as its price had it.
